# Reordering written instruction lists around the tenth to twelfth weight pieces of a fused scan and gated MLP

## The chip, the cores and the metric

The kernel runs on one core of a Trainium2 chip. The metric is the device time of one execution in microseconds; before the change the median of three runs is 338.92 us (338.63 to 339.2). All times in this document are microseconds unless marked otherwise.

## The reference

Two stages follow each other. The first is a gated linear recurrence with 4 batches, 8 heads, 768 steps, head size 32 and state size 16, computed in chunks: within a chunk an intra-chunk product, between chunks a carried state. The second is a gated MLP over the 3072 tokens (width 256, hidden width 1536), in float32:

```python
log_a = np.log(np.clip(a, 1e-06, 1.0))
L = np.exp(cum[:, :, :, None] - cum[:, :, None, :]) * causal
M = np.einsum('bhin,bhjn->bhij', Cc, Bc) * L
y = M @ xc + (Cc @ state) * exp(cum)          # per chunk
state = decay_full * state + sum_j(Bc x xc * decay_from_j)
g = x @ w_gate; val = x @ w_val
out = (silu(g) * val) @ w_out
```

## The kernel before, in words

**Tiling.** The 768 steps are six blocks (k = 0 to 5) of 128 steps; with four batches a block is 512 tokens. For each block TensorE computes the scores `S k`, the values and state sums `st k`, and the carried part `y k`; the result is the MLP's input `x`. The MLP's first layer is cut into twelve pieces (f = 0 to 11) of 128 hidden units; `gv k f 0` and `gv k f 1` are its gate and value products. To keep float32 accuracy on a faster number format, each operand is split into a high and a low part, and a product is three passes: high by high, and the two mixed ones. Blocks 3 to 5 use another scheme with fewer products, for which GpSimd first forms sums of weight pieces (the tiles `wt`, `wd`, `wu`, `ws`).

**Weights.** They arrive as 64-bit words that the kernel narrows itself. For one piece i the steps are `raw i` (the load), `mag i` (ScalarE, absolute value), `range i` (GpSimd for pieces 0 and 3 to 17, a clamp), `rest i` (ScalarE), `shift i`, `sign i`, `round i` (VectorE), `wh i` (ScalarE, the high part) and the low part `wl i`. Pieces 0 to 8 of block 0 are multiplied whole, so their `wh` and `wl` are needed only for block 1; their low part is `minus i` on ScalarE, then a transfer `wl i` started by GpSimd that adds the whole to it. From piece 9 on, `wl i` is a VectorE subtraction that needs `wh i`, and the products of block 0 need both. Pieces 12 to 17 are the second layer's (`wo`). In the trace the tiles are called after them: `wg9h` is written by `wh 9`, `wg10w` by `mag`, `range`, `shift`, `sign` and `round 10`, `sg` by a silu (`si k f`) or by its product with the value (`pr k f`), `po` by the second layer's products.

**Order.** A planner (`Plan`) places all steps, engine by engine, by modelled costs and due times (`rank`). For the start of the kernel the order on each engine is written out by hand in `FRONT`; `Plan.fix` turns each list into a chain, so that a step on an engine comes behind its neighbour in the list. What comes behind the lists is left to the planner. Each engine executes its instructions in the planned order, and an instruction whose operand is missing holds up all behind it on that engine. TensorE's list runs to `gv 1 1 0` and has, around the change, `gv 0 8 1, st 1 3, gv 0 9 0, gv 0 9 1, gv 0 10 0, gv 0 10 1, y 1, gv 0 11 0`; the change leaves it alone. `step 1 0` (VectorE) makes the carried state that `y 1` needs, from the state sums that `ap 1 0` (ScalarE) has masked. `("gv", 1, 5, 0)`-like tuples in `add(...)` are the steps that a step needs.

All instructions are recorded under one helper line (L206 in the profile), so the rows are told apart by tiles. ScalarE is ACT there, VectorE DVE, GpSimd POOL, TensorE PE.

Of the kernel before, what the change touches and what calls it, by code (L numbers as in the profile page):

```python
# [17 lines left out]
BATCH, H, S, D, N = 4, 8, 768, 32, 16  # L18
# [10 lines left out]
NF = DFF // P  # L29
# [4 lines left out]
FAST = 3  # L34
# [14 lines left out]
class Plan:  # L49
# [19 lines left out]
    def add(self, engine, cost, run, rank, needs=(), takes=(), uses=(), gives=None, kind=None, lag=0.0, rows=1.0, slack=0.0):  # L69
        engines = [(engine, cost)] if cost is not None else engine  # L70
        self.ops.append(Op(engines, run, rank, needs, takes, uses, gives, kind, lag, rows, slack, cost is None))
# [145 lines left out]
def scan_moe_kernel(ctx: ExitStack, tc, aj, an, bc, xb, wgv, wo, cst, own, first_e, out):  # L217
# [6 lines left out]
    def pool(name, bufs, stack=ctx, **kw):  # L224
        return stack.enter_context(tc.tile_pool(name=name, bufs=bufs, **kw))
# [5 lines left out]
    raw = pool("raw", RAW)  # L231
# [14 lines left out]
    clipped = dram.tile([2, P, NA * W], F32, name="clipped")  # L246
# [300 lines left out]
    xh, xl = {}, {}  # L547
# [383 lines left out]
    rest = {}  # L931
# [29 lines left out]
    def do(f, *a):  # L961
        return lambda *e: f(*a, *e)
# [6 lines left out]
    add = plan.add  # L969
# [25 lines left out]
    for n, ranks in enumerate(IDLE):  # L995
        for i, r in enumerate(ranks):
            need = [("idle", n, i - 1)] if i else IDLE_AFTER[n]
            takes = [] if i else [("at", ("rest", n))]
# [3 lines left out]
    for i in range(NW):  # L1002
# [12 lines left out]
        if not i:  # L1015
            n, gate = slice(0, 2 * P), [("round", 0, "gate")]
            add("DVE", 0.35, do(w_sign, i, n), r - 3.9, [("shift", i)], gives=("sign", 0, "gate"))
            add("DVE", 0.35, do(w_round, i, n), r - 3.3, [("sign", 0, "gate"), ("rest", i)], uses=[("raw", i)], gives=gate[0])
        n, c = (slice(2 * P, 4 * P), 0.35) if not i else (slice(0, 4 * P), 0.6)
# [75 lines left out]
    for k in range(NB):  # L1095
        r = due(k)
        SLACK = min(k / 2, 1.0)
        z = -5 if not k else r + LEAD[min(k, 3)]
        L, E, BC, XB, CZ, TT = ("L", k), ("E", k), ("bc", k), ("xb", k), ("Cz", k), ("T", k)
# [39 lines left out]
        S = [("S", k, p) for p in range(NP)]  # L1139
        y = [("y", k, i) for i in range(2 * K if k else 6)]  # L1140
        for bs in [(b,) for b in range(BATCH)] if not k else [range(BATCH)]:
            b, more = bs[-1], bs[0]
            n = len(bs)
            add("PE", 0.43 if n == 1 else 1.14, do(scores, k, bs), z + 3.5 if k else -1.9 + 0.1 * b, [("Cz", k)] + ([("S", k, more - 1)] if more else []) + ([("s1", k - 1, NF // 2 - 1, 1)] if k > FAST else []), takes=[] if more else [("at" if k else "mm", i) for i in S], uses=[*S, CZ], gives=("S", k, b), kind="f", slack=SLACK)
            if not k:
                add("PE", 0.2, do(sums, 0, bs), -1.5, [("bt", 0), *([("st", 0, more - 1)] if more else [])], takes=[] if more else [("at", i) for i in st], uses=st, gives=("st", 0, b), kind="f")
        done = [("S", k, BATCH - 1)]
# [11 lines left out]
        uses = [L, E, XB, BC, *y, TT]  # L1159
# [38 lines left out]
    for k in range(FAST):  # L1198
        xs = [(t, k, i) for t in ("xh", "xl") for i in range(2 * K if k else 2) if k or t == "xh" or not i]
        for f in range(NF):  # L1200
# [9 lines left out]
            gv = [("gv", k, f, m) for m in range(2)]  # L1210
# [13 lines left out]
    for k in range(NB):  # L1224
        prev = None
        for n, (m, t, fs) in enumerate(sums_of(k)):
            b = ("po", k, m, t)
# [62 lines left out]
shift 0, sign 0 gate, round 0 gate, sign 0, round 0, range 1, shift 1, sign 1, round 1, range 2, products, shift 2, sign 2, round 2,  # L1290
pr 0 0, shift 3, sign 3, round 3, pr 0 1, shift 4, sign 4, round 4, step 0 1, shift 5, pr 0 2, sign 5, round 5,
shift 6, sign 6, round 6, pr 0 3, shift 7, sign 7, round 7, shift 8, sign 8, pr 0 4, round 8, L 1 0, L 1 1, L 1 2, pr 0 5,
L 1 3, shift 9, bt 1, sign 9, M 1 0, pr 0 6, M 1 1, M 1 2, M 1 3, round 9, pr 0 7, wl 9, shift 10, sign 10, round 10,
pr 0 8, wl 10, ce 1, step 1 0, shift 11, sign 11, round 11, pr 0 9, wl 11, pr 0 10, xh 1 0, xh 1 2, xl 1 0, xl 1 2, xl 1 1, xl 1 3,
step 1 1, shift 12, pr 0 11, sign 12, round 12, wl 12
""",
# [1 line left out]
by batch, Cz 0, mag 0, E 0, rest 0, ap 0 0, written, ap 0 1, xf 0, xf 1, xf 2, mag 1, xf 3, xf 4, xf 5, rest 1, mag 2, rest 2, si 0 0,  # L1298
mag 3, rest 3, mag 4, rest 4, si 0 1, mag 5, rest 5, written e, mag 6, rest 6, xh 0 0, si 0 2, mag 7, rest 7, Cz 1, si 0 3, mag 8,
rest 8, xh 0 1, wh 0, minus 0, si 0 4, minus x 0, minus x 1, mag 9, rest 9, wh 1, minus 1, wh 2, minus 2, wh 3, si 0 5, raw 12, wh 4,  # L1300
mag 10, rest 10, wh 5, wh 6, wh 7, wh 8, si 0 6, raw 13, mag 11, si 0 7, rest 11, minus 3, minus 4, wh 9,
si 0 8, mag 12, rest 12, rest 13, minus 5, wh 10, ap 1 0, ap 1 1, si 0 9, raw 14, wh 11, si 0 10, raw 15, minus 6, minus 7,
xh 1 1, xh 1 3, minus 8, rest 14, si 0 11, raw 16, si 1 0, Cz 2, wh 12, si 1 1, mag 13, raw 17, hh 0 0, si 1 2, hh 0 2, rest 15,
si 1 3, wh 13, si 1 4, mag 14, rest 16, si 1 5, rest 17, si 1 6
""",
    Pool="""
clipped, range 0, range 3, range 4, range 5, range 6, range 7, range 8, wl 0, range 9, xl 0 0, wl 1, range 10, wl 2, wl 3, range 11,
wl 4, wl 5, wl 6, range 12, wl 7, wl 8, range 13
""",
    PE="""  # L1310
# [68 lines left out]
```

## Time and profile before

| what | value |
|---|---|
| median of three runs | 338.92 us (338.63 to 339.2) |
| the profiled execution, its own time | 340.3 us |
| its span, first to last instruction | 338.5 us |
| PE busy | 330.9 us, 98% of the span |
| DVE busy | 232.9 us, 69% |
| ACT busy | 174.1 us, 51% |
| POOL busy | 178.9 us, 53% |
| mean granted TensorE clock | 0.999 of 2.4 GHz |

PE is busy nearly all of the span, so the table alone says little about where time could be lost; the busy time of a PE is modelled from overlapping matmuls, and a stretch has to be read by its own rows.

### The profile page before, as it was taken

How to read it: one execution, taken by the hardware profiler on the slowest of the kernel's cores; microseconds unless marked ns; L12 is line 12 of the kernel's file. 1: busy time of each engine (PE TensorE's matmuls, PEld its weight loads, DVE VectorE, ACT ScalarE, POOL GpSimd, SP SyncE). 2: the span in 40 equal slices, each digit the busy share in tenths (PEclk: the TensorE clock that was granted, in tenths of full speed). 3: DMA queues.
4: the chain of work that ended last, by engine and by line, in shares of the span. 5: the costliest groups of instructions: out<-in, count | busy, mean ns of one | idle time of the engine just before them, and what ended most of it. 6: DMA issues, size and time to landing. Idle time of an engine off the chain costs nothing.

```text
span 338.5 us, 8445 instructions
## 1 busy us (share of the span) xinstructions
PE 330.9 (98%) x3531; PEld 277.1 (82%) x3531; DVE 232.9 (69%) x411; ACT 174.1 (51%) x319; POOL 178.9 (53%) x162
## 2 busy tenths in 40 slices
PE   7999988999999999999999999999999999999996
PEld 5645746888887888888888999878999978999995
DVE  7999889888789991566299776745896833376600
ACT  4796965745245532555372576341657341656411
POOL 2385833522102208977979997541377541368450
PEclk9999999999999999999999999999999999999999
DMA  7799976991000761000182100008400000100001
GB/s 245 257 395 171 319 185 151 301 247 43 1 2 2 199 179 63 1 2 2 36 214 67 62 2 0 4 9 225 145 3 3 3 2 2 62 2 0 2 0 64
DMA packets 9989, 31.06 MB, mean 92 GB/s; under 512 B 1311, under 2 KB 2111, under 8 KB 9311
## 3 DMA queue, kind: packets, MB, share of 16 engines
q1 hardware_dynamic: 7192, 24.23, 24.1%
q0 software_dynamic: 1440, 2.88, 4.7%
q10 hardware_dynamic: 1319, 3.41, 3.2%
q8 instruction: 28, 0.46, 0.6%
q14 instruction: 10, 0.08, 0.1%
HBM read 24.28 MB, written 3.35 MB: 82 GB/s over the span
## 4 chain that ended last, share of the span: by engine, by line
PE 80%; DMA 7%; POOL 4%; DVE 4%; ACT 3%; issue 2%; ACTq 0%; DVEq 0%; POOLq 0%
PE po L206 26%; PE gv L206 21%; PE pq L206 21%; DMA wg11r<-in_wgv 6%; PE y L206 4%; PE r L206 3%; PE S L206 2%; POOL wt L206 2%; PE a L206 1%; POOL ws L206 1%; DVE wg10w L206 1%; DVE wg1w L206 1%; DMA rows<-in_aj 1%; DVE wg2w L206 1%; POOL wg9l L206 0%
## 5 line engine op out<-in xcount | busy, mean ns | idle before, releaser
L206 POOL TENSOR_TENSOR pl<-hp,ph 128x512 fp32r<-128x512 f32 x36 | 46.0, 1292 | 27.9 <-PE po L206 23.9
L206 POOL TENSOR_TENSOR sp<-sp 128x256 f32<-128x256 f32 x36 | 28.6, 796 | 32.2 <-ACT sp L206 29.8
L206 DVE TENSOR_TENSOR pq<-pq,sp 128x512 f32<-128x512 f32 x36 | 25.0, 696 | 20.1 <-PE pq L206 20.0
L206 ACT COPY sp<-pq 128x512 f32<-128x512 f32 x36 | 21.1, 586 | 22.7 <-PE pq L206 21.8
L206 DVE TENSOR_TENSOR_SCAN L<-L,dj 128x520 f32<-128x520 f32 x20 | 26.9, 1380 | 6.2 <-DMA L<-clipped 6.2
L206 ACT ACTIVATE sg<-gv 128x512 f32<-128x512 f32 x36 | 21.5, 596 | 16.5 <-PE gv L206 16.2
L206 ACT COPY ob<-po 128x512 f32<-128x512 f32 (+1 forms) x13 | 7.2, 554 | 38.6 <-PE po L206 38.1
L206 DVE TENSOR_TENSOR sg<-gv,sg 128x512 f32<-128x512 f32 x28 | 19.2, 685 | 11.3 <-PE gv L206 8.6
L206 ACT ACTIVATE hp<-pq 128x512 f32<-128x512 f32 x36 | 20.3, 602 | 12.2 <-DVE pq L206 10.7
L206 DVE TENSOR_TENSOR hp<-pq,hp 128x512 f32<-128x512 f32 x36 | 23.9, 684 | 2.4 <-PE pq L206 1.9
L206 ACT CAST ph<-hp 128x1024 fp32r<-128x1024 f32 x18 | 18.7, 1052 | 9.5 <-PE po L206 6.2
L206 DVE TENSOR_TENSOR sp<-r,sp 128x256 f32<-128x256 f32 x36 | 15.0, 417 | 12.0 <-POOL sp L206 12.0
L206 DVE TENSOR_TENSOR hh<-sg,hh 128x512 fp32r<-128x512 f32 x28 | 20.6, 761 | 0.8 <-ACT hh L206 0.7
L206 ACT CAST hh<-sg 128x512 fp32r<-128x512 f32 x22 | 13.6, 620 | 13.1 <-PE po L206 8.3
L206 DVE TENSOR_TENSOR L<-S,L 128x512 f32<-128x512 f32 x24 | 15.1, 683 | 0.5 <-PE S L206 0.5
L206 DVE TENSOR_TENSOR gv<-gv,sg 128x512 f32<-128x512 f32 x8 | 5.6, 700 | 11.0 <-PE gv L206 11.0
L206 PEld LDWEIGHTS y<-L,xb 64*32 64x32 f32 x768 | 8.8, 108 | 2.6 <-issue 0.8
L206 PE MATMUL y<-L,xb 64*32 64x64 f32 x768 | 10.7, 231 | 0.0
L206 POOL TENSOR_TENSOR wdl<-wd,wdh 128x512 fp32r<-128x512 f32 x6 | 8.2, 1362 | 4.3 <-ACT wdh L206 4.3
L206 POOL TENSOR_TENSOR wt<-wg0h,wg0l 128x512 f32<-128x512 f32 x1 | 1.3, 1291 | 15.9 <-DVE xb L206 15.9
L206 ACT CAST hh<-gv 128x512 fp32r<-128x512 f32 x8 | 4.7, 587 | 9.7 <-DVE gv L206 9.7
L206 DVE SCALAR_TENSOR_TENSOR T<-T,E,y 128x64 f32<-128x64 f32 x36 | 7.5, 276 | 2.8 <-ACT y L206 2.5
(671 smaller groups left out, 1125.8 us busy)
## 6 DMA issues: line engine op xcount, KB each, us to landing
L<-clipped SPq DMA_DIRECT2D x10, 520.0 KB, 15.7
xb<-in_xb SPq DMA_DIRECT2D x6, 768.0 KB, 7.6
bc<-in_bc SPq DMA_DIRECT2D x6, 512.0 KB, 3.5
out<-ob SPq DMA_DIRECT2D x11, 256.0 KB, 4.1
E<-clipped SPq DMA_DIRECT2D x5, 260.0 KB
wg0r<-in_wgv SPq DMA_DIRECT2D x1, 512.0 KB
wg1r<-in_wgv SPq DMA_DIRECT2D x1, 512.0 KB
wg2r<-in_wgv SPq DMA_DIRECT2D x1, 512.0 KB
```

Source lines behind the costliest of these rows:

```text
L206: ins = getattr(self.engine, name)(*a, **k)
```

## The change

Four edits to written orders, and one added need:

- ACT: `minus 3`, `si 0 7` and `minus 4` come ahead of `mag 11`; `wh 9` comes right behind `mag 11`; `wh 10`, `ap 1 0` and `ap 1 1` come ahead of `rest 12`, `rest 13` and `minus 5`.
- DVE: `shift 10` changes places with `wl 9`.
- POOL: `range 11` changes places with `wl 3`.
- PE: the scores of block 2 (`S 2`) now need the last first-layer product of block 1 (`gv 1 11 1`).

```diff
-            add("PE", ..., do(scores, k, bs), ..., [("Cz", k)] + ... + ([("s1", k - 1, NF // 2 - 1, 1)] if k > FAST else []), ...)
+            add("PE", ..., do(scores, k, bs), ..., [("Cz", k)] + ... + ([("s1", k - 1, NF // 2 - 1, 1)] if k > FAST else [("gv", 1, NF - 1, 1)] if k == 2 else []), ...)
 DVE:
-L 1 3, shift 9, bt 1, sign 9, M 1 0, pr 0 6, M 1 1, M 1 2, M 1 3, round 9, pr 0 7, wl 9, shift 10, sign 10, round 10,
+L 1 3, shift 9, bt 1, sign 9, M 1 0, pr 0 6, M 1 1, M 1 2, M 1 3, round 9, pr 0 7, shift 10, wl 9, sign 10, round 10,
 pr 0 8, wl 10, ce 1, step 1 0, shift 11, sign 11, round 11, pr 0 9, wl 11, ...
 Act:
-mag 10, rest 10, wh 5, wh 6, wh 7, wh 8, si 0 6, raw 13, mag 11, si 0 7, rest 11, minus 3, minus 4, wh 9,
-si 0 8, mag 12, rest 12, rest 13, minus 5, wh 10, ap 1 0, ap 1 1, si 0 9, raw 14, wh 11, ...
+mag 10, rest 10, wh 5, wh 6, wh 7, wh 8, si 0 6, raw 13, minus 3, si 0 7, minus 4, mag 11, wh 9, rest 11, si 0 8,
+mag 12, wh 10, ap 1 0, ap 1 1, rest 12, rest 13, minus 5, si 0 9, raw 14, wh 11, ...
 Pool:
-... wl 1, range 10, wl 2, wl 3, range 11,
+... wl 1, range 10, wl 2, range 11, wl 3,
 wl 4, wl 5, wl 6, range 12, wl 7, wl 8, range 13
```

## Rows read from the trace of the kernel before

**Rows 1.** Chain of waits, 54 to 112: start, length, what.
```profile
54.27 3.02 PE gv L206 x12
57.29 1.63 PE y L206 x106
58.92 35.60 PE gv L206 x156
94.52 1.14 PE S L206 x62
...
102.00 1.42 PE y L206 x90
```

**Rows 2.** PE's waits over the span: in total, times, longest.
```profile
PE gv L206 <- ACT wg10h L206: 1.0, 1, 1.0
...
PE gv L206 <- ACT wg9h L206: 0.9, 1, 0.9
PE pq L206 <- ACT hp L206: 0.3, 1, 0.3
```

**Rows 3.** Windows: length, busy PE, PEld, DVE, ACT, POOL (instructions), PEclk, DMA share, GB/s.
```profile
48.80:58.90 10.10, 8.01 (x158) 5.80 (x153) 8.84 (x16) 6.70 (x15) 4.58 (x4) 1.00 0.63 137
58.90:189.00 130.10, 130.10 (x1185) 107.12 (x1184) 97.39 (x162) 64.00 (x123) 68.95 (x57) 1.00 0.34 93
189.00:195.00 6.00, 5.74 (x47) 5.44 (x46) 3.42 (x7) 3.36 (x7) 6.00 (x7) 1.00 0.00 0
```

**Rows 4.** Timeline of PE: start, length, instruction, [idle before <- releaser].
```profile
47.37 0.80 PE L206 MATMUL y<-L,xb 64*32 64x64 f32 x60
...
49.78 0.74 PE L206 MATMUL gv<-xh,wg9h 128*128 128x512 f32 x2 [0.92 <-ACT wg9h L206]
```

**Rows 5.** Timeline of ACT, 46 to 59.
```profile
46.44 0.68 ACT L206 ACTIVATE wg11w<-wg11r 128x512 f32<-128x512 f32 x1 [3.37 <-DMA wg11r<-in_wgv]
47.01 0.58 ACT L206 ACTIVATE sg<-gv 128x512 f32<-128x512 f32 x1
...
48.08 0.62 ACT L206 ACTIVATE wg3l<-wg3w 128x512 fp32r<-128x512 f32 x1
...
49.12 0.61 ACT L206 CAST wg9h<-wg9w 128x512 fp32r<-128x512 f32 x1
...
53.60 0.62 ACT L206 CAST wg10h<-wg10w 128x512 fp32r<-128x512 f32 x1 [1.18 <-DVE wg10w L206]
...
58.13 0.62 ACT L206 CAST wg11h<-wg11w 128x512 fp32r<-128x512 f32 x1 [2.15 <-DVE wg11w L206]
```

**Rows 6.** Timeline of DVE, 31 to 54.
```profile
31.75 0.42 DVE L206 TENSOR_SCALAR wg7w<-wg7w 128x512 int32<-128x512 int32 x1
...
35.20 0.68 DVE L206 CUSTOM_DVE_ANT_0 wg8w<-wg8r,wg8w 128x1024 uint16<-128x1024 uint16 x1
...
45.32 1.88 DVE L206 TENSOR_TENSOR L<-S,L 128x512 f32<-128x512 f32 x3
47.11 0.68 DVE L206 CUSTOM_DVE_ANT_0 wg9w<-wg9r,wg9w 128x1024 uint16<-128x1024 uint16 x1
...
49.76 1.31 DVE L206 TENSOR_TENSOR wg9l<-wg9w,wg9h 128x512 fp32r<-128x512 f32 x1 [1.36 <-ACT wg9h L206]
50.99 1.13 DVE L206 TENSOR_SCALAR wg10w<-wg10w 128x512 int32<-128x512 int32 x1
52.15 0.69 DVE L206 SCALAR_TENSOR_TENSOR wg10w<-wg10r,wg10w 128x512 int32<-128x512 int32 x1
52.87 0.69 DVE L206 CUSTOM_DVE_ANT_0 wg10w<-wg10r,wg10w 128x1024 uint16<-128x1024 uint16 x1
```

**Rows 7.** Timeline of POOL: three clamps (range 8, 9 and 11).
```profile
31.06 1.94 POOL L206 TENSOR_SCALAR wg8w<-wg8w 128x512 f32<-128x512 f32 x1 [3.05 <-ACT wg8w L206]
...
35.30 2.36 POOL L206 TENSOR_SCALAR wg9w<-wg9w 128x512 f32<-128x512 f32 x1 [0.82 <-ACT wg9w L206]
...
49.57 2.25 POOL L206 TENSOR_SCALAR wg11w<-wg11w 128x512 f32<-128x512 f32 x1
```

More of the change, by code (lines that the diff above doesn't have):

```diff
@@ L1143, in scan_moe_kernel @@
             n = len(bs)
-            add("PE", 0.43 if n == 1 else 1.14, do(scores, k, bs), z + 3.5 if k else -1.9 + 0.1 * b, [("Cz", k)] + ([("S", k, more - 1)] if more else []) + ([("s1", k - 1, NF // 2 - 1, 1)] if k > FAST else []), takes=[] if more else [("at" if k else "mm", i) for i in S], uses=[*S, CZ], gives=("S", k, b), kind="f", slack=SLACK)
+            add("PE", 0.43 if n == 1 else 1.14, do(scores, k, bs), z + 3.5 if k else -1.9 + 0.1 * b, [("Cz", k)] + ([("S", k, more - 1)] if more else []) + ([("s1", k - 1, NF // 2 - 1, 1)] if k > FAST else [("gv", 1, NF - 1, 1)] if k == 2 else []), takes=[] if more else [("at" if k else "mm", i) for i in S], uses=[*S, CZ], gives=("S", k, b), kind="f", slack=SLACK)
             if not k:
@@ L1300 @@
 rest 8, xh 0 1, wh 0, minus 0, si 0 4, minus x 0, minus x 1, mag 9, rest 9, wh 1, minus 1, wh 2, minus 2, wh 3, si 0 5, raw 12, wh 4,
-mag 10, rest 10, wh 5, wh 6, wh 7, wh 8, si 0 6, raw 13, mag 11, si 0 7, rest 11, minus 3, minus 4, wh 9,
-si 0 8, mag 12, rest 12, rest 13, minus 5, wh 10, ap 1 0, ap 1 1, si 0 9, raw 14, wh 11, si 0 10, raw 15, minus 6, minus 7,
+mag 10, rest 10, wh 5, wh 6, wh 7, wh 8, si 0 6, raw 13, minus 3, si 0 7, minus 4, mag 11, wh 9, rest 11, si 0 8,
+mag 12, wh 10, ap 1 0, ap 1 1, rest 12, rest 13, minus 5, si 0 9, raw 14, wh 11, si 0 10, raw 15, minus 6, minus 7,
 xh 1 1, xh 1 3, minus 8, rest 14, si 0 11, raw 16, si 1 0, Cz 2, wh 12, si 1 1, mag 13, raw 17, hh 0 0, si 1 2, hh 0 2, rest 15,
@@ L1306 @@
     Pool="""
-clipped, range 0, range 3, range 4, range 5, range 6, range 7, range 8, wl 0, range 9, xl 0 0, wl 1, range 10, wl 2, wl 3, range 11,
+clipped, range 0, range 3, range 4, range 5, range 6, range 7, range 8, wl 0, range 9, xl 0 0, wl 1, range 10, wl 2, range 11, wl 3,
 wl 4, wl 5, wl 6, range 12, wl 7, wl 8, range 13
```

## The prediction

> **What bounds the kernel now.** I read the chain of waits first, then PE's waits, then windows around each, then the timelines of the four engines between 42 and 62. The chain shows one run of first-layer products from 58.92 that lasts 35.60 without a break, and it goes on from there as PE work [rows 1]. PE's waits hold three entries behind the start of the kernel: 0.9 for `wh 9`, 1.0 for `wh 10`, 0.3 for a silu of block 3 [rows 2]. The windows agree: in the 10.10 from 48.80 PE is busy for 8.01, and in the 130.10 behind it for all 130.10 [rows 3]. So PE bounds the kernel nearly everywhere, and what can be won lies in the 10 us before 58.90. Since nothing behind waits for anything but PE's own pace, a microsecond won there should stay won.
>
> Why does PE wait there? ACT stands idle for 3.37 before `mag 11`, until the load of piece 11 lands at 46.44 [rows 5], and `wh 9` sits behind it: `mag 11`, a silu, `rest 11`, `minus 3`, `minus 4`, and only then `wh 9` at 49.12. Its operand, `round 9` on DVE, was done at 47.11 + 0.68 = 47.79 [rows 6]. PE had finished its work before: the values and state sums of block 1 start at 47.37 [rows 4], and the same step in block 2 takes 1.42 [rows 1], so PE was free at 48.79 and began `gv 0 9 0` at 49.78 [rows 4]. DVE in its turn waited 1.36 for `wh 9` with `wl 9` [rows 6], and `shift 10`, `sign 10`, `round 10` stood behind that. So the second wait, `wh 10` at 53.60, has the same root.
>
> **The change part by part.** ACT first. `minus 3`, `si 0 7` and `minus 4` cost 0.62 + 0.58 + 0.62 = 1.82 [rows 5] and fit into the idle 3.37; their operands are products and rounds of long before. `mag 11` keeps its time, 46.44, set by the load. `wh 9` then waits for `round 9`: DVE is busy without a gap up to it (three `mix` steps of 1.88 from 45.32, `round 9` at 47.11 [rows 6]), so 47.79 does not move. `wh 10` began 0.04 behind the end of `round 10` (52.87 + 0.69, then 53.60 [rows 5, 6]); with the same 0.04 `wh 9` runs from 47.83 to 48.44. That is a new wait of about 0.7 on ACT, and behind it stand `rest 11`, `si 0 8` and `mag 12`: at most 0.68 + 0.58 + 0.68 = 1.94, done by 50.4, before `wh 10` can start. PE starts `gv 0 9 0` at 48.79 in place of 49.78: 0.99 won.
>
> DVE next. Steps of this size follow each other by (1.88 - 0.68) / 2 = 0.60 [rows 6]. So `pr 0 7` starts at 47.71, `shift 10` at 48.31. Ahead of `wl 9` it uses DVE's time and no longer waits behind it. Its 0.42 (that of `shift 7` [rows 6]) overlaps the next by the same 0.08, so `wl 9` starts at 48.65, `wh 9` being done, and ends at 49.34; PE wants it two passes into the gate product, 48.79 + 4 x 0.228 = 49.70. `sign 10` starts at 49.25; from its start to the end of `round 10` took 53.56 - 52.15 = 1.41 [rows 6], so `round 10` ends at 50.66, against 53.56, and `wh 10`, now ahead of `rest 12`, `rest 13` and `minus 5`, runs from 50.70 to 51.32. In the run of 156 matmuls one takes 35.60 / 156 = 0.228 [rows 1], so PE has done twelve of them at 48.79 + 2.74 = 51.53 and does not wait: 0.2 to spare.
>
> The twelve of `gv 0 10` alone took 3.02 [rows 1], 0.28 over 12 x 0.228, for both ends of a run. So `gv 0 9` and `gv 0 10` in one take 24 x 0.228 + 0.28 = 5.76, and `y 1` starts at 54.55 in place of 57.29 [rows 1]: 2.74 won in all. The windows give 10.10 - 8.01 = 2.09 of idle PE [rows 3]; the 0.65 between is time in which a first matmul's long tail counts as busy. I take 2.74, from starts to starts, and 2.09 as its lower bound.
>
> Is something late next? `y 1` takes 1.63 [rows 1], so `gv 0 11` can start at 56.18. From the end of `round 10` to the start of `wh 11` were 58.13 - 53.56 = 4.57, set by DVE (ACT idled 2.15 for it [rows 5]); DVE's list between them is unchanged, so `wh 11` runs from 55.23 to 55.85, 0.3 before PE wants it. On ACT three steps come in between that were ahead of `wh 10`: at most 3 x 0.68 = 2.04, inside the 2.15. `ap 1 0` goes with `wh 10`, so `step 1 0` is as early as DVE lets it be.
>
> POOL: `range 11` ahead of `wl 3` can start when `mag 11` ends, at 47.12, in place of 49.57 [rows 7]. It lasts 2.25, so the transfer `wl 3` starts at about 49.4, `wl 4` behind it earlier than before, and `wl 5` later, because `minus 5` moved back. They are wanted by `gv 1 3` to `gv 1 5`, that is four to six times 12 x 0.228 behind `gv 0 11`, from 67 on: nothing. The `wo` loads that ACT issues behind `si 0 9` and `si 0 10` move forward with PE. SP's list is as it was. The added need of `S 2` costs nothing: the scores already ran right behind the last product of block 1, at 94.52 [rows 1]. Behind the written lists the planner places the steps anew; between nothing lost and a gain of the 0.26 that PE still waits at 189 to 195 [rows 3] on one side, and rival three on the other, I take nothing.
>
> One cost the trace does not show directly: `range 11` now runs beside `round 9`, `shift 10` and `wl 9`. Beside it before, `wl 9` took 1.31 and `shift 10` 1.13, where such steps take 0.69 and 0.42: 0.62 + 0.71 = 1.33 too much [rows 6, 7]. Against that, `shift 7` took 0.42 in the middle of `range 8`, and `round 8`, begun 0.10 before `range 9`, took 0.68 while the clamp took 2.36 in place of 1.94 [rows 6, 7]. The bounds for DVE's lateness are 0 and 1.33. `round 9` will again have begun when the clamp starts, and `shift 10` falls into its middle, so the low end is the nearer: I take 0.3, of which 0.2 is covered by the spare time of `wh 10`. That leaves 2.74 - 0.1, rounded to 2.6.
>
> The profiled execution took 340.3 with a span of 338.5; the sum makes that 337.7 and 335.9. It lies 1.4 above the median of 338.92, and what lies around the span is untouched, so I subtract 2.6 from the median: **336.3**.
>
> **The rivals.** One: *the clamp takes DVE's time.* With the whole 1.33, less 0.2 covered, the gain is 2.74 - 1.13 = 1.6, so 337.3. If the clamp went first from the end of `round 9` and held `shift 10` to its end, 47.79 + 2.25 = 50.04, DVE would be 50.04 - 48.31 = 1.73 late and the gain 1.2, so 337.7. For it: the two slow rows; against it: `shift 7` and `round 8`. The Trainium skill, "SBUF — State Buffer", section "Who interferes with whom", has such a rule: VectorE with two SBUF inputs or in its two-port mode shares ports with GpSimd, and whoever issues first blocks the other for the whole instruction. By that rule it would be 337.7; the trace agrees where `round 8` stretched the clamp, and not where `shift 7` ran through one.
>
> Two: *the lead is lost at block 3.* POOL forms the weight sums and is busy for 6.00 of 6.00 between 189 and 195, where PE waits 0.26 [rows 3]. If these sums do not start earlier, PE only waits longer there: 338.9. Against it: they start behind the scans of block 3, whose loads wait until `y 2` has let go of the tiles, and that is PE's pace.
>
> Three, the other side: *the planner puts sums of weights ahead of the first products of block 3.* POOL's seven steps there took 6.00, 0.86 each [rows 3], and PE already waits, so each one more costs PE its whole length. A pair's set has nine; five of them make 4.3, so 338.9 - 2.6 + 4.3 = 340.6. It decides from four steps on (3.4 against 2.6). For it: PE's only late wait is there; against it: the ranks are unchanged.
>
> Four: *`wh 9` hid another wait*, such as the low half of x, whose arrival these rows do not show. Up to 0.99 would go: 337.3.
>
> **How the numbers follow.** The forecast, gains of 2.0 to 3.1 (bounds 2.09 and 2.74, plus the 0.26), holds 0.55; rival one 0.20, two 0.09, three 0.11, four 0.05. The range takes in the forecast, one and four, 335.8 to 337.9, and leaves two and three out: 0.80. About 0.2% (0.7 us) is what can be told from no change here. Faster by more than that: 0.55 + 0.20 + 0.05 = 0.80. Within it: two, 0.09. Slower: three, 0.11.
>
> **What would show it.** Right: the load of piece 11 still lands at 46.4, `wh 9` starts at 47.8, PE shows no wait for `wh 9` or `wh 10`, `y 1` starts near 54.5 and `S 2` near 91.8. Wrong: `shift 10` or `wl 9` over 1 us beside `range 11` (rival one); a wait of PE near 187 to 192 longer than 0.3 (two or three); a wait of `gv 0 9` for something other than `wh 9` (four). A load of piece 11 that lands later than 47 would break the sum at its first step.

## The result, and the profile after

The changed kernel takes 341.0 us (median of 11 runs, 339.5 to 342.69) against 338.95 for the kernel before in the same session: ratio 1.0055, interval 1.0033 to 1.0076. It was forecast 2.6 faster and is about half a per cent slower. Medians from here on leave out the few executions that the chip ran in its slower state (six of the late-load kernels and three of the kernel before).

The profiled execution took 340.24 with a span of 338.5, the same span as the profile of before. That equality hides a gain and three losses that cancel. Here is the chain of waits of the changed kernel from 40 to 120 (start, length, what), to be laid beside [rows 1]:

```profile
49.17 5.71 PE gv L206 x24
54.88 1.63 PE y L206 x106
56.51 35.59 PE gv L206 x156
92.10 1.14 PE S L206 x63
...
108.30 5.95 DMA bc<-in_bc
114.27 0.46 ACT Cz L206
114.90 0.71 ACT Cz L206
115.61 0.52 ACT wo5h L206
```

The two runs of twelve have become one of 24 that lasts 5.71 (I had 5.76), and the run of 156 starts at 56.51 instead of 58.92: 2.41 won against this profile of before. Later the chain leaves PE's own pace from 108.30 to 116.17: the load `bc 3` takes 5.95, ACT's `Cz 3` waits for it, and `wo5h`, which PE wants, stands behind that.

The windows of [rows 3], in the changed kernel (same columns):

```profile
48.80:58.90 10.10, 10.10 (x200) 8.15 (x188) 9.83 (x24) 8.93 (x20) 3.07 (x3) 1.00 0.72 172
...
189.00:195.00 6.00, 4.96 (x38) 4.36 (x37) 3.58 (x7) 2.81 (x6) 5.92 (x7) 1.00 0.00 0
```

PE now fills the first one (8.01 before), but in the 6.00 us at block 3 it idles for 1.04 where it idled for 0.26. PE's waits say the same, the answer to [rows 2] (in total, times, longest; `pq` are the first-layer products of blocks 3 to 5, `hp` the hidden units that VectorE and ScalarE make of them, `sp` the sums on the way, `z` on GpSimd and `w` on VectorE):

```profile
PE pq L206 <- ACT hp L206: 0.6, 1, 0.6
PE pq L206 <- DVE hp L206: 0.4, 1, 0.4
```

The waits for `wh 9` and `wh 10` are gone; those at block 3 have grown from 0.3 to 1.0. ACT's timeline in the changed kernel, beside [rows 5]:

```profile
43.66 0.67 ACT L206 ACTIVATE wg11w<-wg11r 128x512 f32<-128x512 f32 x1
47.36 0.62 ACT L206 CAST wg9h<-wg9w 128x512 fp32r<-128x512 f32 x1 [3.03 <-DVE wg9w L206]
...
50.22 0.62 ACT L206 CAST wg10h<-wg10w 128x512 fp32r<-128x512 f32 x1 [0.58 <-DVE wg10w L206]
...
54.76 0.62 ACT L206 CAST wg11h<-wg11w 128x512 fp32r<-128x512 f32 x1 [0.53 <-DVE wg11w L206]
```

`wh 9` starts behind `round 9`, as worked out. But `mag 11` starts at 43.66, not 46.44, and waits for no load: in this execution the load was in by then.

The two profiles can be split at steps that both have (starts from PE's timeline):

| stretch on PE | before | after | difference |
|---|---|---|---|
| start of `gv 0 11` | 58.85 | 56.44 | -2.41 |
| from there to `S 2` | 35.60 | 35.59 | -0.01 |
| `S 2` to `gv 2 0` (holds wo's steps) | 37.51 | 38.15 | +0.64 |
| `gv 2 0` to the first `pq` of block 3 | 53.88 | 53.86 | -0.02 |
| first `pq` of block 3 to `S 4` | 30.58 | 31.98 | +1.40 |
| `S 4` to the end | 122.08 | 122.48 | +0.40 |

They sum to 0.00. The last row varies from 122.0 to 123.5 between the 19 profiles of this case whatever the order, so nothing is read from it. In ten of them, with either order, PE idles there for 0.5 to 1.1 before a product of block 4's `y`, released by nothing that the profile shows, and the row is 122.8 to 123.5. The +0.64 is the `bc 3` load; it shows in two more profiles (38.26 with the old lists, 38.44 with the changed ones), so it is not shown to belong to the change. The stretch from the first `pq` to `S 4` is the measure that most experiments below use; I call it the block 3 stretch.

### The profile page after: what moved, and what is told of

Read it like the earlier page. It is cut to its first block, busy times and chain, and to the rows that moved or that the text cites. A ratio compares the mean times of both kernels' runs of the same rounds, so it can differ in the third digit from the quotient of the medians.

```text
span 338.5 us, 8438 instructions
## 1 busy us (share of the span) xinstructions
PE 332.0 (98%) x3531; PEld 277.9 (82%) x3531; DVE 232.8 (69%) x411; ACT 174.2 (51%) x319; POOL 180.7 (53%) x162
## 3 DMA queue, kind: packets, MB, share of 16 engines
q1 hardware_dynamic: 7192, 24.23, 23.5%
## 4 chain that ended last, share of the span: by engine, by line
PE 95%; DMA 2%; ACT 1%; DVE 1%; issue 0%; ACTq 0%; SPq 0%
PE gv L206 31%; PE po L206 28%; PE pq L206 23%; PE y L206 5%; PE r L206 4%; PE S L206 2%; DMA bc<-in_bc 2%; PE a L206 1%; DMA rows<-in_aj 1%; ACT Cz L206 0%; PE e L206 0%; PE st L206 0%; DVE pq L206 0%; ACT hp L206 0%; PE rest L206 0%
## 5 line engine op out<-in xcount | busy, mean ns | idle before, releaser
L206 POOL TENSOR_TENSOR sp<-sp 128x256 f32<-128x256 f32 x36 | 29.9, 836 | 30.5 <-ACT sp L206 27.2
L206 DVE TENSOR_TENSOR_SCAN L<-L,dj 128x520 f32<-128x520 f32 x20 | 29.1, 1493 | 5.9 <-DMA L<-clipped 5.9
L206 POOL TENSOR_SCALAR wo4w<-wo4w 128x512 f32<-128x512 f32 x1 | 1.9, 1915 | 15.7 <-ACT wo4w L206 15.7
```

The source lines that it names most:

```text
L206: ins = getattr(self.engine, name)(*a, **k)
```

## Experiments

For most of these kernels the order of every engine is pinned whole: the planner's answer for either kernel was read out, and one is used in one part and the other in another. "Tail" is all that lies behind the written lists. A pinned edit looks like this (cut; `WHOLE_ORDER` has all steps of each engine in order, and each step is tied to its engine):

```diff
     for e, names in FRONT.items():
         plan.fix(e, names)
+    for e, names in WHOLE_ORDER.items():
+        order = [...]
+        plan.follow(order)
```

Ratios are to the kernel before in the same session; they are not the quotients of the medians. The medians of the kernel before were 338.88 in the session of the first four, 338.94 with the swapped GpSimd orders and the later load, 339.48 with the stretches, 339.18 with the held load, the fourth pair and the step moved late, and 339.08 with the step moved back.

**The kernels again, front alone, tail alone.** The first two are the two kernels unaltered; the third has the changed lists and before's tail, the fourth the old lists and the changed tail.

> The kernel before, unchanged, for a second trace of it. Theory A (the front edits win, and the orders that the planner gives out behind the written lists lose): the trace looks as the first one, load of piece 11 at about 46.4, PE waits of 0.9 and 1.0 for wh 9 and wh 10; ratio 1.000. Theory B (the first trace was an unlucky execution, 340.3 against a median of 338.9): the load of piece 11 lands some 2 to 3 us earlier, before 44.5, and the two waits of PE together are under 1.0; ratio 1.000 all the same.

> The changed kernel, for a second trace of it. Both theories: ratio 1.004 to 1.008, PE without a wait from 42 to 60, S 2 near 92. Theory A: the 2.4 us won by then are lost again, the same way as in the first trace: about 0.6 between 107 and 117 (the first product with wo5) and 0.8 or more near 191 (block 3). If the loss sits elsewhere in each execution, it is not an order but the arrival of loads that decides.

> The written lists of the change, and behind them on every engine the order of the kernel before, written out. Theory A: all of the gain and none of the loss, 336.2 to 337.3 (ratio 0.992 to 0.995). Theory B: the gain is what the typical execution of before still has to give, 0 to 1.3 us: 337.6 to 338.9 (ratio 0.996 to 1.000). Theory C (the front edits themselves move the later loads into each other, whatever the order behind): 340 or more, ratio over 1.003.

> The written lists of the kernel before, and behind them on every engine the order that the changed kernel has, written out (with it the scores of block 2 behind the last product of block 1, where they were already). Theory A: the loss alone, 341 to 343.5 (ratio 1.006 to 1.013). Theory B: the same sign, 341 to 342.5. Theory C: within 0.2% of before, 338.2 to 339.6.

| kernel | median us | ratio to before, interval | `mag 11` | `gv 0 11` | block 3 stretch |
|---|---|---|---|---|---|
| before again | 338.93 | 0.9994 (0.9965 to 1.0022) | 41.19 | 55.95 | 30.90 |
| changed again | 339.64 | 1.0022 (0.9995 to 1.0049) | 43.65 | 56.43 | 31.96 |
| front alone | 338.89 | 1.0006 (0.9969 to 1.0044) | 43.28 | 56.03 | 30.61 |
| tail alone | 340.34 | 1.0029 (0.9998 to 1.0061) | 40.92 | 56.41 | 31.83 |

The kernel before, profiled again, shows on ACT:

```profile
41.19 0.67 ACT L206 ACTIVATE wg11w<-wg11r 128x512 f32<-128x512 f32 x1 [0.62 <-DMA wg11r<-in_wgv]
...
47.09 0.62 ACT L206 CAST wg9h<-wg9w 128x512 fp32r<-128x512 f32 x1 [2.67 <-DVE wg9w L206]
...
50.35 0.60 ACT L206 CAST wg10h<-wg10w 128x512 fp32r<-128x512 f32 x1
```

and on PE, with no wait in front:

```profile
48.65 0.73 PE L206 MATMUL gv<-xh,wg9h 128*128 128x512 f32 x2
...
55.95 0.73 PE L206 MATMUL gv<-xh,wg11h 128*128 128x512 f32 x2
```

The wait of 3.37 for the load [rows 5] is 0.62 here, `wh 9` waits for `round 9` in the old order too, and PE waits for neither half. Of the eight profiles here that have the old lists and the load at its old place, the first alone has a late load: `mag 11` waits 3.37 for it there and 0.96 at most in the other seven, where PE waits for neither half. The changed lists alone show no gain (338.89; the interval of their ratio ends 0.3% below 1, about 1 us), and the long block 3 stretch goes with the tail. Theory B holds for the kernel before and, at its upper end, for front alone. The changed kernel again and tail alone come out below what their theories said (1.004 and 341), which suggests a loss smaller than the first result's 2.05.

**One engine's tail.** GpSimd's old order in the changed kernel, and GpSimd's new order in the kernel before.

> The changed kernel, except that GpSimd takes its steps behind the written lists in the order that they had before the change; TensorE, VectorE, ScalarE and the loads keep the changed order. Theory (GpSimd's new order at the pairs of blocks 2 and 3 makes it wait for ScalarE about 1.3 us longer, so the state work of block 3 starts later): the stretch from the first product of block 3's gated units to the scores of block 4 goes back from 31.9 to 32.1 us to between 30.6 and 31.0, the first weight sum of the z step starts under 5 us behind the first product, and the time is 338.4 to 339.4 us, ratio to the kernel before 0.998 to 1.002. Rival (the new order on ScalarE, VectorE or TensorE makes the stretch long, GpSimd's place does not matter): the stretch stays over 31.7 and the time is 339.7 to 341 us, ratio 1.002 to 1.006.

> The kernel before, written lists and all, except that GpSimd takes its steps behind the lists in the order of the changed kernel. Theory (GpSimd's order alone is the loss): the stretch from the first product of block 3's gated units to the scores of block 4 grows from 30.6 to 31.0 us to 31.8 to 32.1, and the time is 339.8 to 340.4 us, ratio 1.003 to 1.005. Rival (the loss sits in the other engines' order, or in both together): the stretch stays under 31.2, the time is 338.5 to 339.3 us, ratio 0.999 to 1.001.

340.05 (1.0033, 1.0002 to 1.0063), stretch 31.77; and 344.2 (1.014, 1.0101 to 1.0179; five executions), stretch 35.98. Both theories fail as put: the first kernel lands in its rival's bounds, the second in nobody's. In the first, GpSimd has the sums ready on time (first `z` 4.33 behind the first `pq`, 5.85 in the changed kernel), and yet the stretch stays long. PE's waits for `hp` come later there, 0.62 at 202.18 and 0.18 at 203.66, and the chain of waits leads back from them over VectorE's `w` and GpSimd's `z` to these rows:

```profile
198.85 0.74 POOL L206 TENSOR_TENSOR wg11l<-wu,wg11h 128x256 fp32r<-128x256 f32 x1 [0.88 <-ACT wg11h L206]
199.54 0.74 POOL L206 TENSOR_TENSOR ws<-wt,ws 128x256 fp32r<-128x256 f32 x1
200.24 0.73 POOL L206 TENSOR_TENSOR sp<-sp 128x256 f32<-128x256 f32 x1
```

GpSimd's old order wants the high half `wg11h` ahead of this `z`, and ScalarE's new order makes it late (argued from that chain, not tested by itself). The engines' orders fit each other; one swapped alone tells little, so the next cut was by time.

**One stretch of the tail, all engines.** The weight sums (132 to 184 us) or block 3's own steps (from 184 on), put into the kernel before or taken back in the changed one.

> The kernel before, written lists and all, except that between the first gated units of block 2 and the first products of block 3 (the stretch of the weight sums, 132 to 184 us) every engine takes its steps in the order of the changed kernel. Theory one (the weight sums of the second half of that stretch come later on GpSimd, which waits for ScalarE 1.3 us longer, and the steps of block 3 start that much later): first product of block 3 to scores of block 4 31.7 to 32.0 us instead of 30.6 to 30.9, first z sum 5.5 to 6 us behind the first product, time 339.8 to 340.4, ratio 1.0025 to 1.004. Theory two (the loss sits in the order of the steps of block 3 themselves): the stretch stays at 30.6 to 31.0 and the time at 338.5 to 339.3.

> The kernel before, with the order of the changed kernel on every engine only from the first products of block 3 on (sums z, their activations, w, ra, rb, cp and the products s1 to s3). Theory one (loss in the weight sums ahead): the stretch from the first product of block 3 to the scores of block 4 stays at 30.4 to 31.1 and the time at 338.4 to 339.3. Theory two (loss in the steps themselves, with the weight sums done on time): 31.7 to 32.0 and 339.8 to 340.4.

> The changed kernel, with the order of before put back on every engine between the first gated units of block 2 and the first products of block 3 alone. Theory one: first product of block 3 to scores of block 4 back to 30.4 to 31.1 us, time 338.4 to 339.4, ratio 0.998 to 1.002. Theory two: 31.7 to 32.0 us, 339.6 to 341, ratio 1.002 to 1.006.

> The changed kernel, with the order of before put back on every engine from the first products of block 3 on alone. Theory one: 31.7 to 32.2 us between the first product of block 3 and the scores of block 4, since the weight sums are late all the same; time 339.6 to 341. Theory two: 30.4 to 31.1 us and 338.4 to 339.4. If both stretches must fit each other, this kernel and the one with the new steps alone are both longer than 32.2 us there, as GpSimd's order alone was (31.8 and 36.0).

| kernel | weight sums | block 3's steps | median us | ratio, interval | stretch |
|---|---|---|---|---|---|
| before + new sums | new | old | 339.92 | 1.0010 (0.9979 to 1.0042) | 31.81 |
| before + new steps | old | new | 339.02 | 1.0005 (0.9980 to 1.0030) | 30.72 |
| changed, old sums | old | new | 338.94 | 1.0003 (0.9972 to 1.0033) | 30.76 |
| changed, old steps | new | old | 340.26 | 1.0030 (0.9993 to 1.0066) | 31.66 |

The stretch falls into two groups, 30.7 to 30.8 and 31.7 to 31.8, by the weight sums alone; the times are too scattered to tell one pair apart (every interval holds 1), but go the same way: beside the 339.48 of the kernel before, the two with old sums are 0.5 lower and the two with new sums 0.4 and 0.8 higher. Theory one is borne out in all four stretches, the last at its edge.

**Smaller: the fourth pair, and then one step.** The changed order from 168 to 184 us only; then a single GpSimd step moved in the kernel before.

```diff
 Pool, kernel before:
-whole 4 1, ws 4 M67, ws 4 52, wsl 3 M5, wsl 3 M2, wsl 3 M1, ws 4 M1
+whole 4 1, ws 4 M67, wsl 3 M5, wsl 3 M2, wsl 3 M1, ws 4 52, ws 4 M1
```

> The kernel before, with the order of the changed kernel on every engine only from 168 to 184 us: the weight sums of the fourth and fifth pair (ScalarE's high halves wsh 3 and hh 2 8, 9; GpSimd's wsl 3, ws 4, whole 5; VectorE's xsum, and xc 3 1 taken over from ScalarE). Theory (these sums alone carry the loss): first product of block 3 to scores of block 4 31.6 to 32.0 us and 339.6 to 340.4. Rival (the shuffles ahead of 168 us, on pairs 1 to 3, carry it or a part): 30.6 to 31.3 us and 338.5 to 339.4.

> The kernel before, with one GpSimd step moved: the sum ws 4 52 (1.3 us) goes from ahead of wsl 3 M5 to behind wsl 3 M1, where the changed kernel has it. Theory (this step is what GpSimd has to do while ScalarE makes the next high halves; without it GpSimd waits): GpSimd's waits for ScalarE between 170 and 176 us grow from 1.7 to about 3 us, the first z sum starts 1 to 1.4 us later behind the first product of block 3, the stretch is 31.2 to 32.0 us and the time 339.4 to 340.4. Rival (the step's place does not matter alone, the coupling to ScalarE's order does): stretch under 31.1 us, time 338.5 to 339.3.

339.71 (1.0015, 0.9987 to 1.0043) with a stretch of 31.75, and 340.07 (1.0039, 1.0018 to 1.0061) with 31.85. One step carries the whole loss of the stretch. GpSimd's timeline in the kernel before, first profile (`wu<-wt` is `ws 4 52`, `wg6l` and `wg7l` are `wsl 3 M5` and `M2`, `sp<-sp` is the first `z`):

```profile
171.53 1.30 POOL L206 TENSOR_TENSOR wu<-wt 128x512 f32<-128x512 f32 x1
173.44 0.74 POOL L206 TENSOR_TENSOR wg6l<-wu,wg6h 128x256 fp32r<-128x256 f32 x1 [0.61 <-ACT wg6h L206]
175.29 0.73 POOL L206 TENSOR_TENSOR wg7l<-wu,wg7h 128x256 fp32r<-128x256 f32 x1 [1.11 <-ACT wg7h L206]
...
190.44 1.44 POOL L206 TENSOR_TENSOR sp<-sp 128x256 f32<-128x256 f32 x2
```

and with the step moved:

```profile
168.12 1.29 POOL L206 TENSOR_TENSOR wd<-wt 128x512 f32<-128x512 f32 x1
171.29 0.74 POOL L206 TENSOR_TENSOR wg6l<-wu,wg6h 128x256 fp32r<-128x256 f32 x1 [1.87 <-ACT wg6h L206]
173.13 0.74 POOL L206 TENSOR_TENSOR wg7l<-wu,wg7h 128x256 fp32r<-128x256 f32 x1 [1.10 <-ACT wg7h L206]
174.01 1.02 POOL L206 TENSOR_TENSOR ws<-wt,ws 128x256 fp32r<-128x256 f32 x1
174.98 1.75 POOL L206 TENSOR_TENSOR wu<-wt 128x512 f32<-128x512 f32 x1
...
189.55 0.74 POOL L206 TENSOR_TENSOR sp<-sp 128x256 f32<-128x256 f32 x1
```

The step used to fill the time in which GpSimd waits for ACT's high half `wg6h`: that wait is 1.87 without it and 0.61 with it. Behind `ws` it costs its full length, and GpSimd has no other gap until `z`. The chain of waits of this kernel shows that it reaches PE (start, length, what):

```profile
174.01 1.02 POOL ws L206
175.03 1.70 POOL wu L206
...
187.97 1.62 POOL wd L206
189.59 1.40 POOL sp L206 x2
...
191.36 0.68 DVE hp L206
192.04 0.62 DVE pq L206
...
192.68 0.61 ACT hp L206
...
193.33 1.69 PE pq L206 x12
```

**The step moved back in the changed kernel.**

```diff
 Pool, changed kernel:
-ws 4 M67, wsl 3 M2, wsl 3 M1, ws 4 52, ws 4 M1
+ws 4 M67, ws 4 52, wsl 3 M2, wsl 3 M1, ws 4 M1
```

> The changed kernel with one GpSimd step moved: the sum ws 4 52 goes from behind wsl 3 M1 back to ahead of wsl 3 M2. Theory (the place of this step is the loss): GpSimd's waits for ScalarE between 170 and 176 us shrink from 3.0 to under 2 us, first product of block 3 to scores of block 4 is 30.5 to 31.0 us instead of 31.9, and the time is 338.4 to 339.4, ratio 0.998 to 1.002. Rival (the new order of the high halves on ScalarE is late for GpSimd in any case, as GpSimd's old order in the changed kernel was 31.8): stretch 31.5 to 32.1 and time 339.4 to 340.6.

338.76 (0.9995, 0.9963 to 1.0026), stretch 30.60. The changed kernel's GpSimd:

```profile
169.27 1.31 POOL L206 TENSOR_TENSOR wd<-wt 128x512 f32<-128x512 f32 x1
172.12 0.73 POOL L206 TENSOR_TENSOR wg7l<-wu,wg7h 128x256 fp32r<-128x256 f32 x1 [1.55 <-ACT wg7h L206]
174.36 0.84 POOL L206 TENSOR_TENSOR ws<-wt,ws 128x256 fp32r<-128x256 f32 x1 [1.50 <-ACT ws L206]
175.17 1.74 POOL L206 TENSOR_TENSOR wu<-wt 128x512 f32<-128x512 f32 x1
...
189.89 0.74 POOL L206 TENSOR_TENSOR sp<-sp 128x256 f32<-128x256 f32 x1
```

and with that one step moved back:

```profile
170.78 1.29 POOL L206 TENSOR_TENSOR wu<-wt 128x512 f32<-128x512 f32 x1
172.38 0.74 POOL L206 TENSOR_TENSOR wg7l<-wu,wg7h 128x256 fp32r<-128x256 f32 x1 [0.30 <-ACT wg7h L206]
174.61 0.85 POOL L206 TENSOR_TENSOR ws<-wt,ws 128x256 fp32r<-128x256 f32 x1 [1.49 <-ACT ws L206]
...
188.75 1.42 POOL L206 TENSOR_TENSOR sp<-sp 128x256 f32<-128x256 f32 x2
```

The wait for `wg7h` falls from 1.55 to 0.30, the first `z` starts 4.46 behind the first `pq` (at 184.29) instead of 5.85 (184.04), and PE's waits for `hp` are gone. What lies between `z` and PE is VectorE's first `w`, here in the changed kernel and with the step moved back; the product of `hp` stands right behind it, and PE waits for that (0.45 at 191.74 in the changed kernel):

```profile
190.66 0.42 DVE L206 TENSOR_TENSOR sp<-r,sp 128x256 f32<-128x256 f32 x1 [3.24 <-POOL sp L206]
...
189.52 0.42 DVE L206 TENSOR_TENSOR sp<-r,sp 128x256 f32<-128x256 f32 x1 [1.88 <-POOL sp L206]
```

The time is that of the kernel before within the interval, and not shown to be lower. An earlier `z` does not shorten the stretch further: in the kernel before, profiled again, it starts 2.31 behind the first `pq`, and the stretch is 30.90.

**A load made late.** The first pair issues the load of piece 11 behind `E 1`, the second also makes it wait for `wh 3`; each with the old lists and with the changed ones, before's tail behind both.

```diff
 SP:
-xb 1, raw 11, E 1
+xb 1, E 1, raw 11            (held: raw 11 also needs wh 3)
```

> The kernel before with one edit in the order of loads: the load of the twelfth weight piece (piece 11) is issued behind the load of the exponents of block 1 instead of ahead of it, some 6 us later. Its data should land at about 46 us instead of about 41, as in the first profile of the kernel before. Theory (the change's front edits answer a late load): the magnitude step of piece 11 then waits for the load by 2 to 4 us on ScalarE, TensorE waits for piece 9's and piece 10's halves again by 0.8 to 1.1 us each, the first product of piece 11 starts at 57.5 to 59.0 us instead of 56.0, and the time is 340.3 to 341.8 us, ratio 1.004 to 1.009. Rival (a late load is hidden by other work and the first profile's 2.7 us came from something else): TensorE's waits do not come back and the time stays at 338.6 to 339.4 us.

> The same later load of the twelfth weight piece, with the changed written lists in front and the order of the kernel before behind them on every engine. Theory (with the load late, the negatives and the silu ahead of the waiting step keep VectorE and ScalarE supplied): TensorE does not wait for piece 9's and 10's halves, the first product of piece 11 starts at 56.2 to 56.9 us, and the time is 338.7 to 339.7 us, that is 1.0 to 2.7 us less than the kernel with the later load and the old lists. Rival (the edits do not help even then): the two kernels with the later load differ by under 0.4 us.

> The kernel before, with the load of the twelfth weight piece made to wait for the rounding step wh 3 (about 35.5 us), so that it lands at 43 to 47 us in every execution; its issue stands behind the exponents' load. All other orders as before. Theory (a late load is what the front edits answer): the magnitude step of piece 11 waits 2 to 4 us for the load on ScalarE, piece 9's and 10's halves come late, TensorE waits 0.8 to 1.1 us for each and the first product of piece 11 starts 8.5 to 9.2 us behind the first of piece 9, not 7.3; time 340.5 to 342, ratio 1.004 to 1.009. Rival (TensorE has slack enough): 7.3 to 7.6 us and no wait, ratio 0.999 to 1.002.

> The same held load, with the changed written lists in front and the order of before behind them. Theory: first product of piece 11 7.3 to 7.6 us behind the first of piece 9, TensorE waits for neither half, and the median is 1.0 to 2.7 us under that of the kernel with the held load and the old lists. Rival: the two differ by under 0.4 us.

| kernel | median us (lowest to highest) | ratio, interval | issue | `mag 11`, its wait for the load | `gv 0 9` | `gv 0 11` |
|---|---|---|---|---|---|---|
| later, old lists | 341.10 (337.82 to 341.72) | 1.0027 (0.9988 to 1.0065) | 29.22 | 41.44, 0.40 | 49.12 | 56.42 |
| later, changed lists | 339.69 (337.48 to 341.89) | 1.0003 (0.9973 to 1.0033) | 28.39 | 45.58, 2.18 | 48.74 | 56.04 |
| held, old lists | 340.19 (338.40 to 342.03) | 1.0020 (0.9995 to 1.0045) | 34.21 | 42.88, none | 51.05 | 58.35 |
| held, changed lists | 340.33 (338.18 to 341.64) | 1.0023 (0.9998 to 1.0048) | 31.59 | 48.53, 4.69 | 49.78 | 57.11 |

Here the issue time did not set the landing. Neither profile with the old lists had a late load, so the comparison that was wanted failed on them (the 51.05 has another cause, told below). The first kernel's median lies in its theory's bounds, but its profile is of one of its fastest executions (337.86), so what held the others up is not seen. Both profiles with the changed lists did have a late load, and there the lists do what they were forecast to do. With a wait of 2.18 PE loses nothing. ACT's timeline in the kernel with the held load and the changed lists:

```profile
48.53 0.69 ACT L206 ACTIVATE wg11w<-wg11r 128x512 f32<-128x512 f32 x1 [4.69 <-DMA wg11r<-in_wgv]
```

and PE's in the same execution:

```profile
49.78 0.72 PE L206 MATMUL gv<-xh,wg9h 128*128 128x512 f32 x2 [0.53 <-ACT wg9h L206]
```

A load 2.1 later than that of [rows 5] costs PE 0.53, and `gv 0 11` follows `gv 0 9` after 7.33; with the old lists in [rows 4, 5] it followed after 9.07, and PE had lost 0.92 ahead of `gv 0 9`. In the medians this does not show: 1.41 apart in one pair with overlapping intervals, 0.14 the other way in the other. That the lists save time in the executions with a late load is seen in single traces, and not shown as a gain in time.

## Why the prediction was wrong

**The front mechanism held with a late load, and was not needed without one.** In the changed kernel's profile the order on ACT and DVE gave what the sum says: `wh 9` directly behind `round 9`, `wh 10` at 50.22 (forecast 50.70, all of it earlier by the 0.46 of `round 9`), no PE wait, `y 1` at 54.88 and `gv 0 11` at 56.44 (forecast 54.55 and 56.18; this execution's first product started at 15.22, 0.34 later than before's 14.88). But the old lists gave the same where the load was in time: in the kernel before, profiled again, `wh 10` starts at 50.35, and `gv 0 11` 7.30 behind `gv 0 9` (7.34 in the changed kernel). What the lists are for shows only in the two profiles above in which the load was late.

**First failed step: "so I subtract 2.6 from the median".** The term behind it, "`mag 11` keeps its time, 46.44, set by the load", was one execution's. The 2.6 was worth what the late load cost there; I had noted that this execution lay 1.4 above the median and took the gain from the median all the same. In the kernel before, profiled again, the load did not hold PE up and `gv 0 11` started at 55.95 without any change. Measured worth of the front in the median: 338.89 against 338.88, nothing, with up to about 1 us either way not excluded (0.9969 to 1.0044).

**Second failed step: "Behind the written lists the planner places the steps anew; ... I take nothing".** It cost about 1.2 in the block 3 stretch (31.7 to 32.0 against 30.6 to 30.9), by one GpSimd sum that came to stand in another place. The mean ratio of the seven measurements with the new weight sums (changed kernel twice, tail alone, new sums, old steps, fourth pair, one step) is 1.0029, that of the five with the old ones and the load at its place (before again, front alone, new steps, old sums, step moved back) 1.0001: about 1 us between them. What remains up to the first 1.0055 (1.0033 to 1.0076) I do not explain; the same kernel's second measurement, 1.0022 (0.9995 to 1.0049), overlaps it. A slip beside these: 2.74 and the 0.26 make 3.0, not 3.1, which moves the range's lower end to 335.9 and decides nothing.

**"A microsecond won there should stay won" held**: front alone reached `S 4` at 213.56 against 216.42 in the first profile, 2.86 earlier, with a lead of 2.82 at `gv 0 11`.

**The rivals.** *One (the clamp takes DVE's time)* was not put to the test in the changed kernel's own profile: there the load was in time, and the clamp was over at 46.34, before `round 9`. It was in the kernel with the later load and the changed lists, beside [rows 6, 7] (DVE's rows, then POOL's):

```profile
46.61 0.91 DVE L206 CUSTOM_DVE_ANT_0 wg9w<-wg9r,wg9w 128x1024 uint16<-128x1024 uint16 x1
48.04 0.52 DVE L206 TENSOR_SCALAR wg10w<-wg10w 128x512 int32<-128x512 int32 x1
...
46.36 1.91 POOL L206 TENSOR_SCALAR wg11w<-wg11w 128x512 f32<-128x512 f32 x1 [4.85 <-ACT wg11w L206]
```

`round 9` took 0.23 too much and `shift 10` 0.10, together the 0.3 that I took and not the 1.33 of the rival, and PE waited for nothing. So the rival is refuted at its price. With the held load the clamp ran from 49.32 to 51.23 and `wl 9`, begun at 49.76, took 0.71. By the blocking rule of the Trainium skill ("SBUF — State Buffer", section "Who interferes with whom") the clamp, begun first, would have held `wl 9`, which has two SBUF inputs, to its end; this trace does not agree. Why `wl 9` and `shift 10` took 1.31 and 1.13 in the first profile [rows 6] stays open. *Two (the lead is lost at block 3)* is refuted by front alone, which kept its lead to `S 4`; that its median is the rival's 338.9 is luck, since in most executions there was no lead to lose. *Three (the planner hurts block 3 through GpSimd's sums)* named the right place, engine and sign and a time, 340.6, that is near; its mechanism was wrong. No sum was added ahead of the first `z`: the same ones came 1.3 later because a filler had left a wait. I gave it 0.11. *Four (a hidden wait for `wh 9`'s neighbours)*: in the changed kernel `gv 0 9` follows the values and state sums of block 1 without a wait, so it is refuted.

## What to carry to other kernels

A wait for a load in one profile is a sample, not the kernel's habit: when that execution lies above the median, take a second profile before pricing the wait, and do not take the gain off the median. Where a planner fills in what the written lists leave open, an edit early on can re-deal steps far behind it, and the price can sit where another engine has little slack; compare the planned orders of both kernels, or pin the old one behind the edit. A step that has no hurry may still be doing a job, as filler in front of a step that waits.

## What the runs showed of the hardware

**TensorE doubles its pace at a time that varies.** The instructions of the tile `gv` from 15 to 22 in the changed kernel with the old sums (count, then least, middle and most ns of one):

```profile
L206 PE MATMUL gv<-xf,wg0w x8: 592/986/1222, 15.7 to 20.9; 128*128 128x512 f32 x8
```

and in the changed kernel profiled again:

```profile
L206 PE MATMUL gv<-xf,wg0w x8: 592/592/697, 15.2 to 18.3; 128*128 128x512 f32 x8
```

The same product takes up to 1222 ns in the one and 592 in the other. In four of the 19 profiles those eight products of `gv 0 0` took 5.38 to 5.77, in the others 3.70, and there `gv 0 9` starts 35.6 to 36.0 behind `gv 0 0` instead of 33.9 (34.5 and 34.9 where PE waited for `wh 9`): about 2 us lost, which is why the held load with old lists shows 51.05. The granted clock is 1.00 (of 2.4 GHz) from 9 to 24 us in both, and PE was busy for 3.00 of each 3.00 us there, so the difference has to be read from the durations; that the lower level, 1.2 GHz, is behind it fits the factor of two and is not shown. The Trainium skill ("TensorE: Matmul & The Clock Gate", section "Seeing it yourself") warns that the recorded clock events are not reliable; these rows agree as far as they go. It occurs with either order of the weight sums, so in the times it adds to the scatter that hides a 1 us effect in a dozen runs.

**A load's landing varies by several microseconds without any change.** Piece 11, issued between 23.5 and 25.3, was in by 40.9 to 42.1 in some executions and came at 46.4 in another; held back to 34.21 it was in before 42.88, and issued at 31.59 it came at 48.5.

**GpSimd's sums slow down beside VectorE's scans.** In the first profile of the kernel before the scans run from 180.49 to 187.70. The sum of 128x512 that takes 1.29 alone took 2.22 to 2.23 there, and one of 128x256 1.67 instead of 0.73, each about 0.93 more whatever its size. It is seen with either order, so it is not the cause here, but it moves the first `z`: with four such sums ahead of it `z` starts 4.60 behind the first `pq`. In the kernel before, profiled again, VectorE waits 2.94 for a load of exponents ahead of the scans, not 0.55; two sums ahead of `z` meet the scans, and it starts 2.31 behind.
